# Issuing the second pieces of q and k ahead of a distance table, with new orders for all engines

## The chip, the cores and the metric

The kernel runs on one core of a Trainium2 chip. The metric is device microseconds (us) of one execution; a median of several executions is quoted. Executions of this program scatter more than the change is worth, so runs are also told apart by the mean clock granted to TensorE, which every execution records: "clean" below means a mean clock of 0.998 or more.

## The reference, cut to what matters

Attention with a window of 128 positions and a distance bias, over 8 batches, 8 heads, 576 positions and 64 dimensions, and behind it a two-layer MLP with h·cos(h) between its layers:

```python
scores = scale * np.matmul(q, k.transpose(0, 1, 3, 2))
rel = pos[:, None] - pos[None, :]
bias = slopes[:, None, None] * (-np.abs(rel))[None]
mask = (rel >= 0) & (rel < 128)
attn = softmax(np.where(mask, scores + bias, -1e9))
x = (attn @ v).transpose(0, 2, 1, 3).reshape(4608, 512)
h = x @ w_in                    # 512 -> 2048
out = (h * np.cos(h)) @ w_out   # 2048 -> 512
```

## The kernel before: the parts concerned

POOL issues all casting loads (float32 in memory, bf16 on chip). It also builds two small tables at the start: an identity, which TensorE needs for transposes, and the distances, from which ScalarE makes eight masks. q and k of the first batch come in two pieces each; q's first piece comes over SP without a cast and is cast by VectorE and ScalarE.

```python
        def distances():
            op("pool", lambda e: e.iota(dif[:, :, :], ...), w=["dif"], occ=450)
            op("pool", lambda e: e.affine_select(dif[:, 0, :], ...), r=["dif"], w=["dif"], occ=430)
            op("pool", lambda e: e.affine_select(dif[:, 1, :], ...), r=["dif"], w=["dif"], occ=400)

        def masks():
            for h in range(H):
                op("act", lambda e, h=h: e.activation(EM[:, h, :], dif[...],
                    ACTF.Exp, scale=slopes[h]), r=["dif"], w=[("EM", h)], ...)
        ...
        load_first_q()
        warm(9, 512, "warm")
        load_qk("k", k, 0, 0)
        distances()
        identity()
        load_qk("q", q, 0, 1)
        load_qk("k", k, 0, 1)
        constants()          # memsets on VectorE, among them those of v's buffers
        load_v(0, range(2))
        load_w_in(0)
        load_v(0, range(2, NBLK))
        masks()
```

What an engine does in which order is not the order of this source. A packed table holds a start for each of the 2,762 operations and, for 50 copies, the engine; operations are sorted by it, and the waits follow from the data:

```python
        raw, n = zlib.decompress(base64.b85decode(STARTS)), len(self.all)
        for i, o in enumerate(self.all):
            code = (code + 256 * raw[i] + raw[n + i]) & 0xFFFF
            o.start = code >> 1
            if len(o.eng) > 1:
                e = "dve" if code & 1 else "act"
                o.fn, o.eng = o.fn[e], (e,)
        self.order = sorted(self.all, key=lambda o: (o.start, o.seq))
```

The softmax here doesn't subtract the row's maximum and nothing guards it: scores larger than these inputs give would overflow.

## Time and profile before

| | value |
|---|---|
| Time | 304.05 us median of 3 (303.7 to 304.66); 303.8 us of 5 with two later runs |
| Span of the profiled run | 301.0 us, TensorE clock 1.000 |
| TensorE idle ahead of 17.2 us / 17.2 to 57 / 57 to 281 / behind | 4.55 / 0.18 / 1.38 / 2.78 us |

The profiled run took 302.76 us, a microsecond less than the timed ones. That was no reason to doubt its order of events.

### The profile page before, as it was taken

What the parts mean: (1) busy time and instruction counts of PE and PEld (TensorE: products, weight loads), DVE (VectorE), ACT (ScalarE), POOL (GpSimd) and SP (SyncE); (2) the same over time, 40 slices, a digit from 0 to 9 for tenths busy, and PEclk for the clock granted to TensorE, in tenths of its full rate; (3) what the DMA queues carried; (4) which work ended last, traced back from release to release, by engine and by line L of the source; (5) the groups of instructions that cost most, each with busy time, mean ns of one, the idle gap of its engine ahead of it and who ended that gap; (6) DMA issues with size and microseconds to landing.
All of it is one profiled execution on the core that took longest, in us unless ns stands there. A gap on an engine that the chain in (4) does not pass through costs nothing.

```text
span 301.0 us, 7132 instructions
## 1 busy us (share of the span) xinstructions
PE 292.1 (97%) x2897; PEld 199.4 (66%) x2917; DVE 244.1 (81%) x511; ACT 210.1 (70%) x304; POOL 94.9 (32%) x122
## 2 busy tenths in 40 slices
PE   7789999999999999999999999999999999999996
PEld 3478745546774588547898886468655865666685
DVE  3787888679977998999978989898878976886871
ACT  6977777487877686787768866888666955744431
POOL 6930992058969301870195014000000000000000
PEclk9999999999999999999999999999999999999999
DMA  7999999999999999999699989645014004310123
GB/s 140 183 200 211 206 169 145 143 130 238 158 138 206 145 156 157 202 166 126 132 141 134 168 85 134 140 84 122 11 53 116 10 2 113 107 35 2 35 89 122
DMA packets 148064, 38.02 MB, mean 126 GB/s; under 512 B 133696, under 2 KB 146752, under 8 KB 148032
## 3 DMA queue, kind: packets, MB, share of 16 engines
q0 software_dynamic: 99344, 18.10, 78.9%
q1 hardware_dynamic: 48688, 19.47, 32.8%
q8 instruction: 23, 0.38, 0.5%
q14 instruction: 9, 0.07, 0.1%
HBM read 36.70 MB, written 9.44 MB: 153 GB/s over the span
## 4 chain that ended last, share of the span: by engine, by line
PE 93%; DMA 4%; POOL 1%; issue 1%; DVE 0%; ACT 0%; ACTq 0%
PE ps L738 36%; PE ps L879 34%; PE ps L762 5%; PE ps L823 5%; PE ps L506 5%; PE ps L593 3%; DMA vp<-in_v_dram 3%; PE ps L596 2%; DMA ob<-in_q_dram 1%; PE ps L700 1%; POOL vp L329 1%; PE ps L451 1%; PE ps L497 1%; PE ps L580 1%; PE ps L582 1%
## 5 line engine op out<-in xcount | busy, mean ns | idle before, releaser
L738 PE MATMUL ps<-xT,w_inb 128*128 128x512 bf16 (+1 forms) x557 | 126.9, 355 | 0.8
L744 ACT ACTIVATE cos<-ps,halfpi 128x512 f32<-128x512 f32 x128 | 82.3, 687 | 39.9 <-PE ps L738 24.3
L748 DVE TENSOR_TENSOR gT<-ps,cos 128x512 f16<-128x512 f32 x128 | 83.0, 686 | 21.4 <-ACT cos L744 20.3
L738 PEld LDWEIGHTS ps<-xT,w_inb 128*128 128x128 bf16 x576 | 55.3, 98 | 39.7 <-DVE gT L748 2.0
L538 ACT ACTIVATE p<-ps 128x768 bf16<-128x768 f32 (+1 forms) x64 | 55.6, 915 | 10.7 <-PE ps L506 7.8
L329 POOL DMA_DIRECT2D vp<-in_v_dram x40 | 34.0, 880 | 66.7 <-PE ps L596 50.9
L879 PE MATMUL ps<-wsum,gT 128*128 128x256 f16 x256 | 48.8, 273 | 0.1
L562 DVE TENSOR_TENSOR p<-p,emask 128x512 bf16<-128x512 bf16 (+2 forms) x96 | 41.9, 460 | 3.5 <-ACT p L538 3.0
L879 PE MATMUL ps<-w_outb,gT 128*128 128x256 f16 x256 | 41.8, 273 | 0.1
L879 PE MATMUL ps<-wsum,gsum 128*128 128x256 f16 x256 | 38.2, 273 | 0.1
L879 PEld LDWEIGHTS ps<-w_outb,gT 128*128 128x128 f16 x256 | 24.6, 98 | 8.3 <-issue 0.5
L339 POOL DMA_DIRECT2D qnat<-in_q_dram x30 | 25.4, 894 | 14.9 <-DMA qt<-qnat 14.9
L879 PEld LDWEIGHTS ps<-wsum,gT 128*128 128x128 f16 x256 | 24.2, 98 | 7.3 <-issue 0.6
L339 POOL DMA_DIRECT2D knat<-in_k_dram x30 | 25.6, 921 | 7.8 <-issue 5.2
L879 PEld LDWEIGHTS ps<-wsum,gsum 128*128 128x128 f16 x256 | 24.5, 98 | 5.2 <-DVE ob L903 0.2
L879 PE MATMUL ps<-w_outb,gsum 128*128 128x256 f16 x128 | 26.2, 273 | 0.0
L593 PEld LDWEIGHTS ps<-vp,p 128*128 128x128 bf16 x256 | 16.2, 97 | 5.5 <-issue 1.5
L593 PE MATMUL ps<-vp,p 128*128 128x65 bf16 x256 | 18.3, 193 | 1.5 <-DMA vp<-in_v_dram 0.8
L506 PE MATMUL ps<-qt,kt 64*128 64x128 bf16 (+1 forms) x320 | 18.8, 239 | 0.8 <-ACT kt L468 0.6
L899 ACT ACTIVATE qrows<-ps 128x512 f32<-128x512 f32 (+1 forms) x18 | 9.9, 550 | 12.3 <-PE ps L879 12.2
L596 PE MATMUL ps<-vp,p 128*128 128x65 bf16 x192 | 17.1, 193 | 0.0
L823 PE MATMUL ps<-w_outb,gT 128*128 128x512 f16 x64 | 16.9, 380 | 0.0
(80 smaller groups left out, 338.6 us busy)
## 6 DMA issues: line engine op xcount, KB each, us to landing
out_dram<-ob SPq DMA_DIRECT2D x32, 256.0 KB, 3.0
vp<-in_v_dram POOLq DMA_DIRECT2D x32, 128.0 KB, 8.6
qnat<-in_q_dram POOLq DMA_DIRECT2D x24, 128.0 KB, 10.6
knat<-in_k_dram POOLq DMA_DIRECT2D x24, 128.0 KB, 12.2
w_inb<-in_moe_w_in_dram POOLq DMA_DIRECT2D x4, 512.0 KB, 9.7
w_outb<-in_moe_w_out_dram POOLq DMA_DIRECT2D x4, 512.0 KB, 21.1
out_dram<-ob SPq DMA_DIRECT2D x8, 128.0 KB, 1.7
qrows<-in_q_dram POOLq DMA_DIRECT2D x1, 576.0 KB, 14.4
```

The source lines that it names most:

```text
L329: op("pool", [lambda e, t=t, rows=rows: e.dma_start(vp[b % 2][0:rows, t, :, 0:64], v[b, :, 128 * t:128 * t + rows, :].rearrange("h p d -> ...
L339: fns.append(lambda e, t=t, rows=rows: e.dma_start(nat[which][b % 2][0:rows, t, :, :], src[b, :, 128 * t:128 * t + rows, :].rearrange("h p ...
L506: ins = e.matmul(ps[:, banks[x], c0:c1], keys_ap(b, x, pr, kc), query_ap(b, x, pr, qb, 128 * nb), start=True, stop=True)
L538: op("act", lambda e: e.activation(P[i][:, :, 0:hi], src_[:, :, 0:hi], ACTF.Exp, scale=0.125), w=held + [("P", i)], occ=920 if G else 691, ...
L562: op("dve", lambda e, p=p, m=m: e.tensor_tensor(p, p, m, ALU.mult), r=[("P", i), ("EM", h0), ("EM", h1)], w=[("P", i)] if n != 1 else [("P ...
L593: ins = e.matmul(o, P[i][:, x, d0:d0 + 128], V[:, kc, h, 0:65], start=True, stop=not two)
L596: ins = e.matmul(o, P[i][:, x, p0:p0 + 128], V[:, kc - 1, h, 0:65], start=False, stop=True)
L738: op("pe", lambda e, kc=kc, c0=c0: e.matmul(ps[:, bank, c0:c0 + n], w_in[:, kc, 128 * fc:128 * fc + 128], xT[:, kc, (r0 + c0) % XR:(r0 + c ...
L744: op("act", lambda e: e.activation(cosb[ci][:, :], ps[:, bank, :], ACTF.Sin, bias=halfpi[:, 0:1]), r=["halfpi"], w=[("B", bank), ("cos", c ...
L748: op("dve", lambda e: e.tensor_tensor(gT[gi][:, fc, :], ps[:, bank, :], cosb[ci][:, :], ALU.mult), r=[("cos", ci)], w=[("B", bank), ("g", ...
L823: op("pe", lambda e, t=t, fc=fc, bank=bank: e.matmul(ps[:, bank, :], gT[gi][:, fc, 128 * t:128 * t + 128], w_out[:, fc, :], start=(fc == 0 ...
L879: op("pe", lambda e, t=t, fc=fc, bk=bk: e.matmul(ps[:, bk, 256 * t:256 * t + 256], lhs(fc, t), rhs(fc), start=first and fc == 0 and (last ...
```

## The change

The intent is to have the DMA engines supplied earlier: q's and k's second pieces are issued right behind the identity, and the distance table, which only the masks need, moves behind them. A new table of orders was searched for this.

```diff
         load_qk("k", k, 0, 0)
-        distances()
         identity()
         load_qk("q", q, 0, 1)
         load_qk("k", k, 0, 1)
+        distances()
         constants()
...
 STARTS = (
-    "c-oy-4RBLc7S2lxT%Iys&+bUL4K=-eREdvR$|Ftk@{+dDG!%%4ONa<1RB<XGcAzd=...
+    "c-o~_3v?7k7M%_O>$I}lyrVd&jB%(mF^)}$p`BmNBm)V<BtVRC3?U#pXoN{bfe~0_...
```

The second hunk may reorder every engine and changes the engine of 20 of the 50 copies.

More of the change, by code (lines that the diff above doesn't have):

```diff
@@ L30 @@
 STARTS = (
-    "c-oy-4RBLc7S2lxT%Iys&+bUL4K=-eREdvR$|Ftk@{+dDG!%%4ONa<1RB<XGcAzd=`B^Hu{8ZiHZ-uQ;cKiW%1ckLIGs}YF2"
-    "#AU-u&lG{=<Yg*E24uf{YkRtB~6<))WW{Wym#NZ=bm@YcfNB@3_>hwNM7A5Lu^n-n=r67DUKOpg1#Gz{}LKW)eQY67zVUo?v"
-    "%z-%orlwg2Y}l`JQ|gqA9NtgVBIL!O(gYuVU9NyV`E#8uj|K5=+7niwWIoT|pXp1|92yCjKVqXSxtbsJ15_MuRaSh#F(U4~A"
-    "aXz?R;U0c}0sg;em8l1NG*3Fo3hA`GDmk{-J$lGrs!QmGN^vF;nr%(&x%u|sG{SQFZN#}?}?$ZYFZB~4(A^p>PDJ%P}GD}6w"
-    "q1Jo0~zToKV9=(cxoeb&C7$KD}X%=G1WOv3Rv<nHb&>|$1+LKhe4lL4C(yug?v_uJmQt^v)d7VH`FhtU<MXwXlRDva|$<Woi"
@@ L36 @@
-    "1Y>)*ae{QpXzw~I47hC6A6REs&=tMh`sdj-(5l}vMnlgJ>AC6TSx@aq-!dU}SNPepKfi0Z#@!UPST}c#LR<1|rXG{f(Up#jN"
-    "H@WaMxBX<%m@M<(-k`U1#Lj<|3S#K@)df2D5F!7O2}9mA%!#@!!=8~9PMgJ8A5CKMrKD6rG!$n(?er(f{L+7e?b`rUAcY^ru"
-    "E03wHI$@gPQwj^c``9jyNttnvS7ISNyqp?(S+CvG%UDu{-3p&VLpC(_>J}^<yBUA$b+1xAmFg&VeZOO@s7K6-oJSr;cFM|IE"
-    "bN`b~3s0MY(SB6<yymLBf(c0BR7BYKswC-i9HJ$EC$EX3j+wYRqsp{Gx%FGSL`dY_A?B`(^>_`I5I%Fx)iL%GD`*Ckh8p2d{"
-    "y%An-ZV~Z|~-@3x@FY@~rnhHESs{<#(GlcJF2rZ`2y*Kf)!Jift6}eq_+v~^c%TLEI_$j+|k<&L<jsXSpD8HG$ku~S-Jrxf*"
@@ L41 @@
-    "MmLtSoI-j<8tyvD+W2=veT(ON>3L<A_nDC^ZS!|EP2W=p%~F;<$`0je$LG!u<mKiO5D5`s#&aw6C;sZxPk=xX5N1*%1ejf<Y"
-    "_<BN2+R$P*k`{<WFj$&yWfbMFp+>sohEXwA2O9{1V|N=t4wM;eTx&Zf&QlSZQU-~W2O557quKuJjV!71;Dhpn9(T=Z7x>@iL"
-    "x*en@n1Sh$h_^lRECTw|9DD58nNs^^4yf7_QiCALl#EyyK?qgr{<LWVPqpr<;9Db4sV_#No$^HZO0A)WnMM?XIlPZ1w9KGlI"
-    "EJ1Z1T7;_#Owf!$RIQm#=4a{HdkjXbQcz8D-L;cV(V2*F8+C@AO_<@CS6bpPn2DwI^yO78dBfCt>bk1z0r763ozF8CTep7CY"
-    "|9PB<jK;`GBRsrT$eMI6QYa>G7s8_Qpchit}C2dlEU3?7YNmsNV_+yGqYo{E3rM^cMpGEyg&_~^BDfLmm_Avy54{Cqmz%8o4"
@@ L46 @@
-    "c(77yRjOEtcbc0s$vf@D(PeD6`SDS3H<v4qZeRz@b4Nj$L>0d?zpM~fCdEHGe?lRYN+xL?n}q?tAp8B*{>($G!dsfRHaEJOZ"
-    "~WI$MZuitSpgz4!pu?#xX21n1So=GuU)3V;>?J1f=H&1NP;PWgoK&Sic}={R-~UHk~r#y5+ZV7;d~+?ZOoqMM>;D|5r|EODK"
-    "iMG2?t6}Eu}J8)HfO6z0B%>dgr5X>0pt%21L5hd(YBS8)tgA&;W3CWe^luTZc*bvpO5^3$-OOSGYP0gSBZl)N*ds)&!|!QMF"
-    ")@aqT-AWO?e7TkR9fluf(0WUKrH+d1JGtE04fujlYs=`>8pI+iuRpnORA;6mjzl;)htu4ru9v3k1Bkekc~_Hse^=6d_`KNNy"
-    "I`>R{w%Yd@dzW7$U=IOWmtNeA2XTvMVsi$izYW_X(XeCoHW*r>_K{ORfjEG8*Bmv8M|Msr6D6;}4xpY2*I3DXDenetCaT?-U"
@@ L51 @@
-    "W<o|gS>>XH2s5w^HeUQ@ww)ElO@t|ksFHW|sF~`>y@|whc|Z1*(|Ye7Gk@Sg?|iseIYk{C1=^(E1i)u#o3JD;(^ep*r+)Auq"
-    "dcI^RVX;LdnBvWsP6Y!CClt_vcma<IViDspW_TI-*e*l3+A=uv%HS`#_m|&)P8b%v1@<bM#VpT-jYIi;$<V^$L2LGaf0;Zr@"
-    "2sEE!&^6e{H>Q42}G=1hAag=^5ddI&PV_+vRsWRM%7&u$pOtYS>2>5b!W4=mZAXFy~qz-893s=?DWif{=%_6m_snp&}v&MPf"
-    "?=I?Nd)uLFrQE8iuOl1clVdu5T92gm{95<`%;@i9~0C5i^{qg<WLWvYYB)yETkNL;JtSedJlouftSJ{RGVjXrBrhXRpH(C#F"
-    "41jWXNN#M>6EPg_=s}Ji336U-89f%Xbn&Ij+Cb}7ZN75d(N?0%WwZDzzdV3^b(UxEj&^_j*ld0&2^GxRIFMxQ^5c+c8R{Nu7"
@@ L56 @@
-    "S~donmwuR~wJH7~HFLa<B}Y!#{X@38&*Vy<1vRkmYpy)L%X+~6*E?Y(U2S#TVW;Iw?xdsXxz7>mSL+{Mf8v&a<J_sk7d#bG0"
-    "v^2~6K1OwITA*+iwW?v_P2Su8A+H2Osf+SiIC6`O%<Y!s-6zfhaos}UNNBNW;A1V=o<x7M}BfpS2f2o7SeD2rRR}~90^H*JA"
-    "aSOqux1d)l_QHBG|#2oDWH!kbU9+L`U&%=L%}>K~1~bD$yX8I4G<{`<8NPrnVn-xcXiQnW~QE%8wpx7}C|I&OYC?J^Xl~!<p"
-    "HD)LXcw5MoDW<Rb|enOn=iew%4De0iwy=oULwrrim%+>^2=2Vco?eE;_spI^=#nHwLGt4Kgegcc98;VZVblaNf84jaA*Gbg8"
-    "z&~z3-6kTy<f<CcK3mFHgR&Q@aw21{oed+<d`e8G^$~CtK^570<T^=&_AOuXLx`|}NjdG?DBjW03Ks}a;w;@dRrEB1iZNB36"
@@ L61 @@
-    "+fUH-+Aiv!SE3H)`T#fsRB|})vih*&{YeU99kxJ4*rvYArS<MNa<JxQwfF)Dn>MZisCE7_SsxE`8_HW6cNIGh&0JHrSt;Li="
-    "!5&=9k{hFTiRnjQ~1mB5&Mq+c<?ul3n$00T7Chlv8<$c&e_v?7pjUkAidd$!`?p$z*v$VNSZhXxO5{%qKtKGGT><x*r!q^i#"
-    "60gY(r*zcr0f!c0MIc?Dww=l3J;{L1K)ZJZaUZMnU#P*}qd=7V_EaSBwGf=IRCodv@u_<p$tCE&IIE;wf7fa@X<0^LL}%JD6"
-    "3Wj#^vA3e+K0Um+Q84zjf~)lJO99nKw92f>r|iKklT_s<DRSdGm!18oi4@=lJkda9VaE`&p}LY7F_RPR<~9AN<#WLTLp%W}F"
-    "f;bhVHc~n7K2RwvT_+%_uJE<1KL{XS%TCMopdiaVj&JLdAJVBUZ$5{!A6~Y|EIbZ0-&$uKr8CwAI-Bch~)XMehTn^P-T~@Tz"
@@ L66 @@
-    "TBQA!ZBs1j`wZ|t+;=uusm`{_hxnEa60hRwh}}USR|mh|xGi5@_u{<W7WHt5!RyDKsISIh_CdoU#wWi4Z*iaV<5L{lO#Ol*`"
-    "2k0!Z92LQIzJ`dJDIN9Y+Vm-QIW`5F{t?6JLNgKn_}g97G+r<BN(`c1&)7&)Dv-B$u+fc)*lbN3W?;N?#y^=ZY+1NPIavH1D"
-    "ykZaPD`xzl)DJBEHi(`zimL{|^uA{Jj"
+    "c-o~_3v?7k7M%_O>$I}lyrVd&jB%(mF^)}$p`BmNBm)V<BtVRC3?U#pXoN{bfe~0_v#^HGLJXi7CH^2HBJ28J`M7FSR7Auzi"
+    ">`PMD)?FS99B_8k|mkxecj0<nM?@iHl(NORn@C{_uY4^O@bCR#hzFzDnu_Z4LqqOM~tp!(zK43spEgAsq-12zXU-OPMJDJyG"
+    "FE5pIUcU(+yf&S3rvpGe%5F#&6Q;gj4l!eBQRcM$dPi)^96f>ViXy3f+TUK??Ex_?UZoi}ePy7=cHHq$I;%TQatPH1&QW2^O"
@@ new lines @@
+    "tae}Jjg)c4bK!)TW`!4wg?M|;lc-=g*2U5i1e^=S8%0HKFT5F)~9wCJ7oq;rJU(~YU$Ap5fjNoV4^-LPssAdUm*EFfy}tAw*"
+    "d7Qeoe16pEPbn`{)>S^6W#(6tWlXONuxu9u6i;kjBnHaLa0G)FilG}P);_)*m7dcDZ9r(4!VE#V{ro|J?*tM+_n`EuW83*8="
+    "$!EHk4mzc89Ua&%w4zMuwl?8htQz#+Ux8CER0I<_)th;J>Pw`Lb42=R3H`3^f7EoIqwzE~c!-XZP4ReKaJtJ=QY6~LYnxudT"
+    "2iY{OZ;n3P_N#|Cq;gFg(m<lm=Y-(O(<wBR?0%mA|%X7w3yCfF~!QV>om#H_IMI@6sj?)>zYk!F?DkAoO~M8`pY?ZK}&+x#p"
+    "eL?Gq5G$8t8fpv5GY%jK*Icf~h~Pi>cRu_HIiL6+I)IF9yFxuY^QixA&I&<kLd$ghu1FUq~cRzZN0h4<e8h!7$s-eSb&KX-E"
@@ new lines @@
+    "t)p|FI+vN_$?oiFI0cikzBBz_SjUWbCQs`K<h*V?FHeB)@5gwsZPom=a?pW<gldkI%GAqK4vFwSNxxl}uTDU+G;{NSb*k0(P"
+    "ue9_kjYX@!n!8R%o@C5?1%#Evp&F1C<({f&|`0Ww%oY7al^-RnAKA+Fy#@B)XK5wroS^Ag2O-gFoo%RzFNRV%~o4>i{LS<7%"
+    "C7V_^mZgr8TIC_G!+9UbZx(uvjCNqxk#;JzFvt7Sq?-p%gk$PuG}qE#|FL!Rdk5wDUrKIDL_#)9-3V?{PAb5bpD#*i$x=e&U"
+    "Z!Q(0+RVer9Mey#ijf`4-pl#nfX_SjewayrcxlF+iv%hDr`}6-lK}TfGHC7Ei1%nB}6PW^Vx(_oJMN-ql}^twxYy)t-gZ~f@"
+    "VHIbQXxE)JAy<j){a3%5S;$#FoOA6_dYuYF2YJ=)T`MuHa+JZ?!!sy-gQ2R@j_^&Hv=@Mq-pHsah(p-uc(;@AQ~cu0BrvWr2"
@@ new lines @@
+    "wel@2(KV?yeE@<Mvtaj`t?OC89~_pBBd1@+dz%a0ZWWfh8nNq#r@3lLSXwg**^=1IT+W_cvY0&7kaG((t45RjIFAEb|G<$RC"
+    "9;ABs@gsSDa^o5zO8MuP+9l8fTL@BY?@tdovPfpL<99mbFoHt%%Px-uuB`CJ?JE#gpd7CBh*Lip8#Ncz$DdQjd{fimDQ<Bx3"
+    "i8la~m1}QjAla_lh&!?T$@NaJ{g`d^NICzC!?X6kOdnj7KLW-Me?tunuAb|FadMMdv?jaIfwnbrO1Z-Ua{B&2U_t;w|M>cwl"
+    "Qr2(-C5bo-9!XEbz;ZMJe`GALM#&K2Fzs2Yg;jim{c(~%S<~P8BBDG7EcB>5pjuObE37>BBi=2GIS19=&8#BwiGH4*NKoT>R"
+    "z1+k@p6bO*yTQ15WQ0P?_p|`hJk=_*by0sg6&%e~y0zANe_BVSX1vW94^-WQ1chm0<d3D*;&8yRrcB$kQZx(G2hJK`mf;&p*"
@@ new lines @@
+    "s$tM|TK%2?i7Spuu~x(Ds~RHFIU<o?|@lO0IgZ*x9NS4_G?XUHhue^M*eMMs`lt1~2(wx(^_&=|SxgwBu=sozmc)xNcM%j)|"
+    "a)HZzR<?s$k8=ILwOuAvrvA~OgP}-j0(|51VdCr-A>{a5Uo-if&&j5u|(gi3oLL{lKOh14e1FuvP-K+I6nt|_9Std|UC4yxp"
+    "i&!|iv49K{P8wbeNM$N-Yd*YiyAu}?5M_6k?x#%NTM9Z!c7P;jB8rG#{!Q6X8ybB_(e~^bu1RyC+IuBZWfFe^-&s@F<9p0|F"
+    "G~<&-a-{Tncij6!;s0pP!QuO*B46)b6tg8m%Yzo)mr)F1N&aHO|Q=z0rS)UR=smq_8(l%!4<bv?|!x62#2X@uVfburqk&Vhb"
+    "*TK9cCW=C!5`|ry;j;1i0GUKMe!}wdEDTKVCevrosJb)u<ci?UZRJ%McdxLAn@7iJW8Lgk_(8XBx;on8-x)TSTP9LyWjHkdm"
@@ new lines @@
+    "~D`f##aM3{_u>4*0D#Vj`>Pn}|c1gny7ncajd!ACp*+uf1^#Ixk6o)%qU_`OvBC8Cv2F?J$iolBb_PKO1aqdxwwU-CiCPET&"
+    "$2oy3&A@-cH!!Re5D8$F75h61@h?U<?j0kLuUr9t8#oeuZIVzMcUW`9ZsG`#$C+{c85KP?dE?kKGz--NA$Ve)xR<04MhmEJ2"
+    "+~B;-;+y?%$<t7o`e?(}bzd~jbior9TkJ&_*3kLskS;l>{a>{<=jQS~^pO$pNMp6lxt=~3oIes=6*U%Au2135^`33T&X0oY_"
+    "l9XViju{A>~lOdR%WbzQxBQD+PU?_CKBI^q@&mku(6re)I$+0_>;0ZD`wed7sGaG-O~>o=;S#R>*lN|6<^nNiC-n@wEPTpua"
+    "?ivT_w%pvtdESK`-|)**@L{Okw=D@&>T+M{vHKJ5))w@*Nb_())obsc!Fwj3UhMNEY-nMGbAekq-;%p0E3M=LgLXIlxu0JEv"
@@ new lines @@
+    "%Hc&bC*xG4!qm|0{IMuY519wlG0)#khvuZ4vp&4RNoZOw`)mpj*vug?xOI2)RNBI4HIjGzuX6|pwWbC7Tps7J>Mjbh5Kqd;W"
+    "Z6*~pwAQ*M%Hdsi;n3q^+mac_v1P01IkTQOs&ORLoH~wURG~eq4X7g0*k}y>CC^;VA$q-&1R`1VD52;Y1P`B|!bEwwG1uA3k"
+    "H_^;>S>AgV17&<=h^dS}4}Pim-Hr1UydD+;3)%A?fQyiEZ8rT<N%5<y;yv^X!^&S{fOYe?J9jj`^rloHE!*Z%i@e#(9JW^Z`"
+    "U;pcMP2Sf;os#+8#6C>cT*dswwjZ=up2>xIom@G6!Zu&2s+%g!MJfdK>(uCMnl?kqlXj$@zVm7C8~&itfon5Ra4r=6p@nZ;`"
+    "%b10zpztgDI}lqKW`6E+e^&R?HJsb3qBfM_GJ5qiWqhCo(8y{JSM|>lm*C8q^67%`f+iDdB|=*A%ny_lBzKQT0`}lkxPudVF"
@@ L69 @@
+    "o+(wbcFCG3+jJHJA$$NFglH95z7p+u2RZzx;k+*_Ml56*J3MW$zETS=&PiA^jGVk((_e(L{{(V(i!ZYkZA;`$!zjw<-+QZI!"
+    "SEN}XW$Y6#{6j4t;^@I5p2ADr87Uwb<^GL5a{<(okkcb|f1frVqeyKhev9S{sFD2A8wMq#+wU5sYQk#9;vKr=Rk5}UD$M`s_"
+    "vc&pWUbx7gG4-L^u$1xGPr*_s-gU?iwIA`rMZ4>)-WE{HqWm%%Jjh&YhVCz7eEHW((8?dE`^|3a^&`S&i4_)=LU!qdrsi)*v"
+    "Em06a`h8fh*I&QsqS?WT7bk7QGH-f$&jn3txO`Iq8efyVc@b<;y<{BVjsh19d`?PuIdFtenn|PxFhF6`p?4~!4NokPfRh=KO"
+    "4TC81rC%Ojy`4_CHg`1$z"
 )
```

## The prediction

> **What bounds the kernel now.** I read the page first: the busy shares, then the chain that ended last.
>
> ```profile
> PE 292.1 (97%) x2897; PEld 199.4 (66%) x2917; DVE 244.1 (81%) x511; ACT 210.1 (70%) x304; POOL 94.9 (32%) x122
> PE 93%; DMA 4%; POOL 1%; issue 1%; DVE 0%; ACT 0%; ACTq 0%
> ```
>
> TensorE is busy in 292.1 of 301.0 us, and the chain runs over it for 93%. The rest, 4% DMA and 1% POOL, must lie at the start, since the change touches only POOL instructions there. So I asked for busy time by stretch, with the cuts at 17.2 us and at later stage borders:
>
> ```profile
> core 0: us, PE busy (x) PEld busy (x) DVE busy (x) ACT busy (x) POOL busy (x), PEclk, DMA share, GB/s
> 0.00:17.20 17.20, 12.65 (x174) 6.68 (x175) 10.13 (x32) 14.17 (x24) 14.80 (x27) 1.00 1.28 164
> 17.20:57.00 39.80, 39.62 (x452) 26.62 (x454) 32.89 (x79) 27.20 (x41) 17.29 (x21) 1.00 1.66 183
> ```
>
> From 17.2 to 57 us TensorE is idle for 0.18 us: the stages behind the start are full. Of its 8.9 us of idle time, 4.55 lie ahead of 17.2 us and 2.78 in the last 20 us; the drain at the end is not touched in the source. The first 1.26 us precede the dummy matmuls that keep the clock up, so about 3.2 us of idle between 5.3 and 17.25 us is all that a better start could give. Whatever makes the dense stretch begin earlier, with the same work done ahead of it, ends the kernel earlier by as much.
>
> The chain in order of time says what the dense stretch waits for:
>
> ```profile
> 5.66 0.28 DVE vp L395
> 5.94 0.29 issue
> 6.23 1.76 POOL vp L329 x2
> 7.99 0.76 POOL w_inb L361
> 8.74 0.84 POOL vp L329
> 9.59 7.57 DMA vp<-in_v_dram
> 17.16 0.09 issue
> 17.25 0.19 PE ps L593
> ```
>
> It is a later tile of v, issued by 9.59 us and landing at 17.16 us. A 7.57 us transfer of 128 KB is no latency: it is the queue in front of it. So the question is whether the DMA engines were ever empty before. The DMA view of the first 18 us, in 40 slices of 0.45 us, answers it:
>
> ```profile
> DMA  0000093999999499999999999999999999999999
> GB/s 0 0 0 0 0 146 86 355 419 282 207 212 101 40 151 193 202 188 196 202 191 156 155 155 170 204 209 207 205 209 200 148 145 154 153 191 205 204 212 205
> ```
>
> There is one hole after the start: the thirteenth and fourteenth slices, 5.4 to 6.3 us, move 101 and 40 GB/s where neighbours move about 200. The first piece of k has drained, and the second piece of q has not begun. POOL's timeline shows why:
>
> ```profile
> 1.33 0.82 POOL L310 DMA_DIRECT2D krows<-in_k_dram  x1 [0.81 <-POOLq L1056]
> 2.24 0.37 POOL L381 IOTA dif<- 128x256 f32 x1
> 2.77 0.29 POOL L385 TENSOR_SCALAR_AFFINE_SELECT dif<-dif 128x128 f32<-128x128 f32 x1 [0.15 <-POOL dif L381]
> 3.20 0.29 POOL L388 TENSOR_SCALAR_AFFINE_SELECT dif<-dif 128x128 f32<-128x128 f32 x1
> 3.44 0.20 POOL L374 MEMSET ident<- 128x128 bf16 x1
> 3.71 0.29 POOL L375 TENSOR_SCALAR_AFFINE_SELECT ident<-ident 128x128 bf16<-128x128 bf16 x1
> 3.95 0.75 POOL L310 DMA_DIRECT2D qrows<-in_q_dram  x1
> 4.70 0.71 POOL L310 DMA_DIRECT2D krows<-in_k_dram  x1
> ```
>
> The reader sees POOL build the distance table and the identity between the issue of k's first piece and that of q's second. ScalarE's rows beside it show the first three masks at 3.53 us, as soon as the table is there (1.03 us for the three).
>
> **What the skill says.** (1) "DMA: Bandwidth & Descriptors", Latency and other measured facts: a software-generated DMA has its first byte after about 1 us. Here it is longer: q's second piece is issued at 3.95 us and packets pick up in the slice that starts at 6.3 us, about 2.3 us later. I use 2.3. (2) The same page, Issuing engines are not separate DMA queues: all issues share the same 16 engines and interleave. The trace agrees: between 4 and 5 us both queues move packets, 154 software and 63 hardware. An early second piece can therefore take bandwidth from q's first piece, but as both software pieces stand in one queue I expect it behind k's first. (3) "Perfetto Trace Analysis", on the GPSIMD lifecycle: time such instructions by the spacing of their starts, not by reported spans. So the table costs 3.44 - 2.24 = 1.20 us, not the sum of its spans (0.95). (4) "ScalarE: Activation LUTs", What ACT_TABLE_LOAD costs: an ACTIVATE with immediates takes 186 ns + 0.833 ns per element and overlaps the next by about 93 ns. For 256 elements that is 399 ns; the trace's median for a mask is 400 ns, and three take 1.03 us. It agrees.
>
> **The change part by part.** Nothing is added or taken away. Two DMA issues pass ahead of three POOL instructions, and a new order with new engine choices for the copies stands in an opaque table.
>
> *Issues earlier.* With the table gone from in front, the identity starts at 2.24 us, takes 3.95 - 3.44 = 0.51, and q's second piece is issued at 2.75 us (1.20 earlier), k's at 3.50. First packets at 2.75 + 2.3 = 5.05 us, while k's first piece still drains until some 5.6. So the hole should close. What it is worth is not the 1.20 us but the work missing from the hole: against 200 GB/s, 0.45 x (1 - 101/200) + 0.45 x (1 - 40/200) = 0.22 + 0.36 = 0.58 us. From there on the DMA engines are backlogged, so all that follows shifts by this: q's second piece from 8.45 to 7.9 us, k's from 10.2 to 9.6, and the tile of v from 17.16 to 16.6. The issues of v do not move in the source order (POOL still does the same work by 5.4 us and then waits 0.81 us for a memset of v's buffer until 6.23); they needn't, as the queue before them is full.
>
> *What it is worth on TensorE.* It waits 0.76 us for that tile just before 17.25, 0.34 us for q's and 0.29 us for k's second piece. 0.58 fits below 0.76: gross gain 0.58 us.
>
> *Table later.* Identity and two issues in front (0.51 + 0.75 + 0.71 = 1.97 us) move its end from about 3.5 to 5.5 us. The three masks that ScalarE did at 3.53 to 4.56, in a time when it had nothing else, must go behind its cast of q at 4.78 to 5.41. From there to the table load at 18.27 us ScalarE has hardly a gap: 0.4 us at 12.96 is the only one named. So 1.03 us of work is added to a full stretch. Some can be taken off: a copy out of PSUM of 0.57 us (128x512) or 0.89 us (128x640) can go to VectorE, which was busy 10.13 of the first 17.2 us and stood idle 1.4 us before its first mask product at 8.87. And ScalarE waits 3.4 us for TensorE in the first 30 us once the first layer of the MLP runs, so later delay can be absorbed. I take 0.15 us as what remains on the path: my estimate between 0 (all moved) and 1.03 (none).
>
> Sum: -0.58 + 0.15 = -0.43 us. In the scale of the timed runs, 304.05 - 0.43 = 303.6; I go to **303.5** as a search that was made for this order should not have ended on a bad start.
>
> **Rivals.** *ScalarE takes the place of the DMA.* The masks push the first exponentials (8.03 us) and the xT copies (15.72) back; then the dense stretch waits for exponentials rather than v. For it: ScalarE's full stretch. Against it: only the first two of eight masks are needed for the first product at 8.87 us, and the rest can fall into later gaps. It would make 303.7 to 304.5. *The transfer is hidden anyway.* The product that the waiting matmuls read also needs VectorE, whose mask multiply at 15.26 lasts 1.28 us, until 16.54. If v comes at 16.6 and VectorE has not moved, the gain is capped at some 0.7 us; that leaves 0.58 standing but bars more. If VectorE is later, the gain goes to zero: 304.0. *The new order changes the full stages.* With TensorE at 39.62 of 39.80 us there is little to win there, but the last 51 us have about 3 us of idle (0.21 and 2.78) and a new order can take or give some tenths. It goes either way: 302.8 to 304.6. *Contention with q's first piece*, which lands at 4.75 us and starts everything: early packets of the second piece could push it back. Against it: they would come at 5.05 us by the 2.3 us above. If not, +0.3 us.
>
> **Range and chances.** The known part gives -0.58 to +0.3 us; the new order widens it by some 0.6 either way; the runs before spread over 303.7 to 304.66. So 302.6 to 304.6 for 8 in 10. 2% is 6 us, more than all idle time at the start together, so faster by 2% is nearly excluded; slower by 2% would need a broken order. Faster 0.01, same 0.98, slower 0.01.
>
> **What would show it.** In the changed trace q's second piece is issued near 2.75 us and lands by 8.0; the hole at 5.4 to 6.3 us is filled; the masks start at 5.4 us or later; v's waiting tile lands near 16.6 and the dense stretch starts with it. If v lands earlier and TensorE is still idle until 17.2 with ScalarE or VectorE named, the second rival holds. If the start gains 0.5 us and the time doesn't move, idle time in the later stages, above all the last 20 us, has grown. The prediction fails if the hole stays because descriptors come later than 2.3 us, or if the search moved v or the weights in the queue too.

## The result, and the profile after

The changed kernel took **303.02 us** (302.86 to 303.51, 5 runs) against 303.8 us (303.7 to 304.66, 5 runs). The ratio is 0.9973, 95% interval 0.9955 to 0.9990. The predicted 303.5 was within half a microsecond and the range held it. Whether it was for the reason given is another question, and the profile after raises it at once.

POOL did what was foretold. This is its timeline after; columns are start, duration, engine, line, operation:

```profile
1.33 0.85 POOL L310 DMA_DIRECT2D krows<-in_k_dram  x1 [0.82 <-POOLq L1056]
2.17 0.23 POOL L374 MEMSET ident<- 128x128 bf16 x1
...
2.71 0.76 POOL L310 DMA_DIRECT2D qrows<-in_q_dram  x1
3.47 0.71 POOL L310 DMA_DIRECT2D krows<-in_k_dram  x1
4.20 0.37 POOL L381 IOTA dif<- 128x256 f32 x1
...
6.00 0.89 POOL L329 DMA_DIRECT2D vp<-in_v_dram  x1 [0.53 <-DVE vp L395]
```

q's second piece is issued at 2.71 us (2.75 foretold), k's at 3.47. The DMA view of the first 18 us, in slices of 0.45 us, shows the hole of 5.4 to 6.3 us filled, 179 and 142 GB/s where there were 101 and 40:

```profile
DMA  0000094999999999999999999999999999999999
GB/s 0 0 0 0 0 137 105 328 400 291 205 200 179 142 142 168 185 185 185 183 182 168 151 149 105 112 152 184 191 198 165 178 160 186 146 153 188 189 205 209
```

But a new dip stands further right, 105 and 112 GB/s around 11 us, where the kernel before had 170 and 204. And TensorE did not gain at the start. Its longest waits after are these (time in all, times, longest):

```profile
PE ps L762 <- DMA w_inb<-in_moe_w_in_dram: 1.7, 1, 1.7
PE ps L416 <- DVE p L413: 1.3, 1, 1.3
PE ps L506 <- DVE kt L469: 1.2, 1, 1.2
PE ps L451 <- DMA krows<-in_k_dram: 0.7, 1, 0.7
```

The wait for v, 0.76 us before, is gone; in its place stands one of 1.7 us for the second quarter of w_in, which landed at 20.5 us. Busy time by stretch (columns as in the prediction) sums it up:

```profile
0.00:17.20 17.20, 13.15 (x180) 7.42 (x181) 10.28 (x34) 12.92 (x22) 15.17 (x27) 1.00 1.26 158
17.20:57.00 39.80, 38.12 (x445) 26.07 (x444) 33.17 (x77) 29.84 (x43) 17.05 (x21) 1.00 1.60 192
57.00:281.00 224.00, 223.97 (x2150) 152.27 (x2149) 189.74 (x384) 160.01 (x225) 62.82 (x75) 1.00 1.11 115
```

Idle ahead of 57 us: 4.05 + 1.68 = 5.73 us, against 4.73 before. Idle from 57 to 281 us: 0.03 against 1.38 us. Two single profiles thus say that the start, which the change was for, became worse and the late stages, where I expected nothing certain, became better. That is what the experiments had to test.

### The profile page after: what moved, and what is told of

The parts are those of the page before. It is cut to its first block, busy times and chain, and to the rows that moved or that the text cites. A ratio compares the mean times of both kernels' runs of the same rounds, so it can differ in the third digit from the quotient of the medians.

```text
span 301.2 us, 7145 instructions
## 1 busy us (share of the span) xinstructions
PE 292.4 (97%) x2917; PEld 199.9 (66%) x2917; DVE 245.1 (81%) x513; ACT 209.1 (69%) x302; POOL 95.0 (32%) x122
## 4 chain that ended last, share of the span: by engine, by line
PE 92%; DMA 5%; POOL 2%; issue 0%; DVE 0%; ACT 0%; ACTq 0%
PE ps L738 37%; PE ps L879 33%; PE ps L823 5%; PE ps L506 5%; PE ps L762 4%; DMA w_inb<-in_moe_w_in_dram 3%; PE ps L593 3%; PE ps L596 2%; DMA ob<-in_q_dram 1%; POOL vp L329 1%; PE ps L451 1%; PE ps L700 1%; PE ps L497 1%; PE ps L580 1%; PE ps L582 1%; PE ps L662 0%
## 5 line engine op out<-in xcount | busy, mean ns | idle before, releaser
L738 PE MATMUL ps<-xT,w_inb 128*128 128x512 bf16 (+1 forms) x576 | 129.0, 355 | 0.0
L879 PE MATMUL ps<-wsum,gT 128*128 128x256 f16 x256 | 48.0, 273 | 0.0
L879 PE MATMUL ps<-wsum,gsum 128*128 128x256 f16 x256 | 39.4, 273 | 0.0
L879 PE MATMUL ps<-w_outb,gsum 128*128 128x256 f16 x128 | 24.9, 273 | 0.0
L593 PE MATMUL ps<-vp,p 128*128 128x65 bf16 x256 | 18.3, 193 | 0.2 <-DVE p L562 0.2
L762 PE MATMUL ps<-xT,w_inb 128*128 128x256 bf16 x128 | 16.3, 273 | 1.7 <-DMA w_inb<-in_moe_w_in_dram 1.7
L506 PEld LDWEIGHTS ps<-qt,kt 64*128 64x128 bf16 x320 | 11.0, 94 | 9.7 <-issue 4.0
## 6 DMA issues: line engine op xcount, KB each, us to landing
knat<-in_k_dram POOLq DMA_DIRECT2D x24, 128.0 KB, 10.4
```

What stands on the lines that cost most here:

```text
L506: ins = e.matmul(ps[:, banks[x], c0:c1], keys_ap(b, x, pr, kc), query_ap(b, x, pr, qb, 128 * nb), start=True, stop=True)
L593: ins = e.matmul(o, P[i][:, x, d0:d0 + 128], V[:, kc, h, 0:65], start=True, stop=not two)
L738: op("pe", lambda e, kc=kc, c0=c0: e.matmul(ps[:, bank, c0:c0 + n], w_in[:, kc, 128 * fc:128 * fc + 128], xT[:, kc, (r0 + c0) % XR:(r0 + c ...
L762: op("pe", lambda e, i=i, fc=fc, kc=kc: e.matmul(ps[:, bank, 256 * i:256 * i + 256], w_in[:, kc, 128 * fc:128 * fc + 128], xT[:, kc, r0:r0 ...
L879: op("pe", lambda e, t=t, fc=fc, bk=bk: e.matmul(ps[:, bk, 256 * t:256 * t + 256], lhs(fc, t), rhs(fc), start=first and fc == 0 and (last ...
```

## The experiments

Twelve runs were made; all gave correct results. Times in us, median and range of all runs; "clean" is the count with a clock of at least 0.998 and their mean.

| Run | chip | median (range) | clean: count, mean | ratio to before (interval) |
|---|---|---|---|---|
| before, beside the next four | A | 304.21 (302.28-305.91) | 7 of 11, 303.82 | |
| after_again | A | 302.69 (302.14-304.52) | 5 of 6, 302.63 | 0.9961 (0.9922-1.0000) |
| undo_issue | A | 302.19 (302.0-303.1) | 5 of 6, 302.15 | 0.9940 (0.9902-0.9979) |
| new_start_old_rest | A | 303.43 (302.9-304.02) | 6 of 6, 303.43 | 0.9977 (0.9942-1.0012) |
| old_start_new_rest | A | 303.18 (302.49-303.67) | 6 of 6, 303.09 | 0.9966 (0.9931-1.0001) |
| before, beside the next four | B | 305.74 (302.57-307.45) | 2 of 11, 302.95 | |
| move_only | B | 304.05 (303.27-304.6) | 6 of 6, 303.99 | 0.9961 (0.9918-1.0005) |
| undo_again | B | 302.51 (302.27-303.4) | 6 of 6, 302.64 | 0.9917 (0.9877-0.9956) |
| after_third | B | 302.79 (301.95-304.75) | 4 of 6, 302.39 | 0.9934 (0.9885-0.9983) |
| undo_v4late | B | 302.20 (302.06-302.7) | 6 of 6, 302.30 | 0.9905 (0.9867-0.9944) |
| before, beside the next four | C | 304.12 (302.96-305.27) | 8 of 11, 303.89 | |
| after_hoist | C | 302.43 (302.05-302.9) | 6 of 6, 302.48 | 0.9949 (0.9922-0.9976) |
| after_hoist_v4late | C | 302.02 (301.87-302.55) | 6 of 6, 302.10 | 0.9933 (0.9905-0.9962) |
| before_fill | C | 304.36 (303.77-304.72) | 2 of 4, 304.25 | 1.0009 (0.9975-1.0042) |
| before_again | C | 305.04 (one run) | 1 of 1 | |

### First, what makes the runs scatter

The kernel before had a mean clock of 0.994 in 4, 9 and 3 of its 11 runs on the three chips, so the ratios of chip B compare mostly slowed runs with clean ones and are not used below. What happens then is in one profile of the changed kernel, **after_again**, whose run took 304.52 us. It is the changed kernel unedited.

> The changed kernel once more, as the anchor for the others of this call and to see how far a profile repeats. All theories: ratio to the kernel before 0.996 to 0.999, 303.0 us. Theory START (closing the hole in the DMA lets the dense stretch begin earlier): TensorE idle ahead of 57 us would be below the 4.7 us of the kernel before. Theory LATER (the start is no better, the new order of the later stages has less idle time): idle ahead of 57 us again near 5.7 us and idle from 57 to 281 us again near 0.

Its busy time by stretch; the third number from the right, ahead of DMA share and GB/s, is the granted clock:

```profile
19.00:20.00 1.00, 0.00 (x0) 0.00 (x0) 0.99 (x3) 0.99 (x2) 0.00 (x0) 1.00 1.27 211
20.00:21.00 1.00, 0.43 (x4) 0.35 (x5) 0.00 (x0) 0.20 (x1) 0.00 (x0) 0.92 1.23 203
21.00:22.00 1.00, 1.00 (x6) 0.71 (x5) 0.00 (x0) 0.00 (x0) 0.00 (x0) 0.50 1.25 208
22.00:23.00 1.00, 1.00 (x9) 0.83 (x7) 0.00 (x0) 0.30 (x2) 0.00 (x0) 0.50 1.23 205
23.00:24.00 1.00, 1.00 (x7) 0.67 (x6) 0.87 (x3) 0.67 (x2) 0.00 (x0) 0.50 1.22 214
24.00:25.00 1.00, 1.00 (x21) 0.91 (x20) 0.62 (x2) 0.28 (x1) 0.00 (x0) 0.87 1.20 225
```

TensorE waited 1.97 us for w_in, and then had half its clock for over 3 us; 0.08 + 3 x 0.50 + 0.13 = 1.7 us of clock are lost. In the other profile of a slowed run (before_fill, below) the clock is lowered for as long, but earlier, from about 17.8 to 21.2 us, behind a wait of 0.72 us for v that had shorter gaps ahead of it. new_start_old_rest waited 1.99 us for w_in and kept its full clock. These are the rows of TensorE behind those two waits, of before_fill and of new_start_old_rest, with the idle time in brackets:

```profile
17.64 0.19 PE L595 MATMUL ps<-vp,p 128*128 128x65 bf16 x1 [0.72 <-DMA vp<-in_v_dram]
```
```profile
20.47 1.16 PE L755 MATMUL ps<-xT,w_inb 128*128 128x256 bf16 x9 [1.99 <-DMA w_inb<-in_moe_w_in_dram]
```

So idle time at the start can cost its own length and, now and then, 1.7 us more, but the length of the last wait alone does not decide it, and what does stays open. The kernel before had the lowered clock on each of the three chips, in 16 of 33 runs, and before_fill, which is nearly the same kernel, in 2 of 4. All the other kernels together, the changed one among them (3 of 12), had it in 4 of 60; move_only had it in none of its 6 runs beside the 9 of 11 on chip B. So it goes with the kernel before, and 1.7 us in a run that has it is twice what the new rest is worth below. Which part of the change avoids it was not tested, and means of clean runs leave it out. The five runs of the changed kernel behind the result above were all clean; of the five of before the clocks are not on record.

The expectation of idle time ahead of 57 us failed in a way that teaches: 57 - 13.72 - 37.83 = 5.45 us, and 224 - 222.97 = 1.03 us later on. At half clock TensorE is busy for longer (the nine matmuls behind the wait took 1.88 us, and 1.16 in the profile after), and the modelled ends of matmuls differ a little from profile to profile. Busy time in two stretches is too coarse here; a mark in the order of work is better. I used the third load of an activation table on ScalarE, which stands between the first MLP stage and the attention behind it at 38 to 41 us.

### Splitting the kernel in time: new_start_old_rest and old_start_new_rest

The two tables were spliced: operations that the first table starts in its first 40 us keep its order, everything else has the other's.

```diff
-        self.order = sorted(self.all, key=lambda o: (o.start, o.seq))
+        # FIRST, REST: the two tables; 1600 of their units are about 40 us
+        for o in self.all:
+            early = FIRST.start(o) < 1600
+            o.key = (0, FIRST.start(o)) if early else (1, REST.start(o))
+            o.eng = FIRST.eng(o) if early else REST.eng(o)
+        self.order = sorted(self.all, key=lambda o: (o.key, o.seq))
```

(The result was written back in as a table of ranks; this is what it holds.)

> All that the new table starts in its first 40 us in the new order, everything after in the old order. START: keeps the whole gain, 303.0 us (ratio 0.997). LATER: no gain or a small loss, 303.8 to 304.5 us (1.000 to 1.002).

> The old order and the old issue order for the first 40 us, the new order for the rest. START: no gain, 303.8 us (ratio 1.000). LATER: keeps the whole gain, 303.0 us (0.997) or a little more, since the old start had 1.0 us less idle time in the profiles.

With before and after_again, on one chip, this is a square of four; means of clean runs:

| | old rest | new rest |
|---|---|---|
| old start | 303.82 | 303.09 |
| new start | 303.43 | 302.63 |

The new rest is worth 0.73 and 0.80 us, the new start 0.39 and 0.46 us. By the scatter of the runs, differences from the corner of both olds (302.28 to 305.91 us) are uncertain by about 1 us and the others by about 0.6 us, an estimate; only the 0.80 stands clear of that. **The larger part came from behind 40 us**, where the move of two DMA issues has no part; a smaller part from the start is likely, but not shown.

The spans confirm the first of these without the scatter of the start. From the third table load to the end, these ACT rows (start, duration) of before, changed kernel, new_start_old_rest and old_start_new_rest

```profile
38.70 1.28 ACT L538 ACT_TABLE_LOAD   x1
```
```profile
39.25 1.28 ACT L538 ACT_TABLE_LOAD   x1
```
```profile
39.15 1.28 ACT L531 ACT_TABLE_LOAD   x1
```
```profile
39.53 1.28 ACT L531 ACT_TABLE_LOAD   x1
```

give, taken from the spans of 301.0, 301.2, 301.7 and 301.4 us: 262.3 with the old rest, 261.95 with the new, 262.55 with the old, 261.9 with the new. Over all profiles, the new rest took 261.9 to 262.0 us in eight of nine (263.0 in undo_again, where TensorE waited 1.0 us for a transposed k of a later batch), the old rest 262.3 to 263.4 in four with a full clock. That gap of some 0.4 to 0.8 us fits the square. The start's part (38.3 to 39.3 us at the mark with the new start, 38.7 to 39.9 with the old, slowed runs aside) overlaps from run to run; the square makes it likely, no more.

### The issue order alone, inside the new orders: undo_issue and undo_again

The changed kernel, with the table put back ahead of the identity on POOL. Nothing else differs, on any engine.

```diff
+        by = {o.w[0]: [] for o in self.all[13:21]}
+        for o in self.all[13:21]:
+            by[o.w[0]].append(o)
+        first = by["ident"][0].start
+        for i, o in enumerate(by["dif"]):
+            o.start = first - 3 + i
         self.order = sorted(self.all, key=lambda o: (o.start, o.seq))
```

> The new order on every engine, with the distance table put back ahead of the identity on POOL alone. START: the hole at 5.4 to 6.3 us is back, k's second piece lands later by about 0.5 us, and the time grows by 0.4 to 0.6 us, to 303.5 us (ratio to the kernel before about 0.999). LATER: what POOL does first is hidden, the time stays at 303.0 us (0.997).

> The new orders with the distance table back in front on POOL, a second time, beside the changed kernel. START: slower than after_third by 0.4 to 0.6 us. ORDER: as fast or up to 0.5 us faster than after_third, ratio to the kernel before 0.994 to 0.997.

> The changed kernel, third set of runs, beside undo_again. Ratio 0.996 to 0.998 by both theories; the time from the third ACT table load to the end 262.0 us within 0.2, as in all profiles with the new order there, against 262.3 to 262.6 with the old one.

On chip A the kernel without the early issue was faster than the changed one (302.19 against 302.69, clean means 302.15 and 302.63), on chip B its clean mean was slower (302.64 against 302.39) and its median lower. Together: **no gain from the early issue** that these runs can see. Weighted by their scatter, the 20 clean runs put that gain between about -0.7 and +0.2 us, an estimate that leaves the predicted 0.58 outside. The early issue was meant to be the cause, and it can be taken out without loss. The third set of the changed kernel put its mark as expected: third table load at 38.30 us, 300.2 - 38.3 = 261.9 us to the end.

Yet the hole was there again in undo_issue (slices of 136 and 65 GB/s) and TensorE's wait for w_in's second quarter had not grown: 1.3 us. Why does filling the hole not help? The DMA between 10 and 12 us, in slices of 0.05 us, first without the early issue (undo_issue):

```profile
GB/s 156 156 148 159 154 151 144 159 164 151 141 159 159 154 154 161 156 159 164 179 179 161 213 174 184 223 138 246 195 192 233 184 225 246 143 266 184 184 205 205
DMA packets 1639, 0.36 MB, mean 178 GB/s; under 512 B 1472, under 2 KB 1639, under 8 KB 1639
```

and with it (new_start_old_rest):

```profile
GB/s 133 120 125 131 125 143 128 136 169 102 182 128 74 123 10 10 64 128 82 95 59 95 120 69 146 169 123 220 133 192 184 184 225 205 143 225 205 184 184 205
DMA packets 863, 0.27 MB, mean 137 GB/s; under 512 B 678, under 2 KB 863, under 8 KB 863
```

The packets under 512 B are v's. By the packets in the traces, with the early issue its first two tiles start about 0.6 us sooner and are nearly through by 10.6 us; then, until 11.2 us, the engines move 10 to 128 GB/s, before the large packets of w_in come at their full rate. Without it v's tiles are through at about 11.2 us and w_in's packets follow at full rate at once. **The hole did not go, it moved**, from 5.4-6.3 to about 10.6-11.2 us (to 11.9 in the profile after). All 14 profiles, old and new orders together, say the same. By 8 us the seven with the early issue have moved 1.27 MB on average and the seven without it 1.15, which is the 0.12 MB of the hole (0.58 us at 200 GB/s); by 12 us 1.87 and 1.85, by 18 us 2.96 and 2.97. What was won at 6 us is lost again by 12 us. The tile of v that the kernel before waited for landed at 17.1 to 17.9 us in the four profiles with the new start and the early issue, and at 16.4 and 16.6 us in undo_issue and undo_again.

The packets in the traces, which no view prints one by one, show what a hole is made of; q's second piece and w_in are told apart by their sizes, 1280 and 1024 bytes. Without the early issue the first 32 packets of q's second piece took 252 to 321 ns each on average, and with it 116 to 148; the first 32 of w_in took 97 ns without it (146 in before_again), and with it 137 to 342. A packet that takes longer counts as busy for longer, so the row of busy tenths can read 9 over a hole.

### The move alone, in the old orders: move_only

```diff
+        for o in self.all[14:17]:                       # the distance table
+            o.start = 193                               # behind k's second issue
+        late = {("EM", 3): 369, ("EM", 5): 397, ("EM", 7): 427}
+        for o in self.all[:60]:
+            if o.w and o.w[0] in late:
+                o.start = late[o.w[0]]
         self.order = sorted(self.all, key=lambda o: (o.start, o.seq))
```

In the old table three masks stand ahead of ScalarE's cast; they were moved with the distance table, or the cast would have stood behind masks that wait for it. v's first issue came at 6.34 us, 0.1 us later than in the kernel before.

> The kernel before with the move alone: distance table behind both issues on POOL, and the three masks that ScalarE did before its cast put between the first exponentials, all other orders and engines as before. START: most of the gain without any search, ratio to the kernel before 0.997 to 0.999 (303.0 to 303.6 us on a chip where before is 303.8). ORDER (the gain is in the new orders of the engines, part in the first 40 us, about 0.4 us after them; the issue time itself gives nothing or costs): ratio 1.000 to 1.003.

Its six runs were all clean: 304.05 us. The kernel before has only two clean runs on that chip, 302.57 and 303.34; over all three chips its 17 clean runs average 303.75. The ratio of 0.9961 fell on the first theory's side, but only as nine of before's eleven runs there had the lowered clock. Clean against clean, the move alone gained nothing that these runs can see; whether it is what avoids the lowered clock, in all six of its runs, is the rival left open above. In its profile the DMA has the same dip (77 and 94 GB/s at about 10 us), and TensorE's wait for v is still 0.9 us.

### Does an earlier supply of v and w_in cure the dip? after_hoist

If the dip is there as the descriptors of v and w_in come no earlier than before, then issuing these earlier should fill it. POOL's first issue of v waits 0.53 us for a memset on VectorE that stands behind a cast; it can go ahead of it.

```diff
+        for o in self.all[21:23]:    # memsets of v's first buffer
+            o.start = 60             # ahead of VectorE's cast of q
         self.order = sorted(self.all, key=lambda o: (o.start, o.seq))
```

> The changed kernel with the two memsets of v's first buffer put ahead of VectorE's cast of q, so that POOL's first issue of v needn't wait for them: it comes at about 5.45 instead of 5.97 us, and all issues behind it too. Theory SUPPLY (the early second pieces only move the hole in the DMA from 5.4-6.3 to about 10.6-11.6 us, as the descriptors of v and w_in come no earlier): that second hole is refilled about 0.5 us sooner, w_in's second quarter lands 0.3 to 0.5 us before the 20.5 us of the changed kernel's profiles, and the clean runs fall from about 302.75 to 302.3 us. Theory BACKLOG (my prediction: the DMA engines are busy from 6 us on whatever is issued): landings and time as after, 302.7 us.

POOL's first issue of v came at 5.58 instead of 6.00 us, so the lever was 0.4 us. The dip was not filled sooner; this is the DMA of the first 18 us:

```profile
GB/s 0 0 0 0 0 123 114 364 423 278 200 212 199 210 202 191 202 202 210 156 156 152 158 96 97 105 143 198 193 163 206 159 156 151 161 173 182 203 209 209
```

The slices of 96, 97 and 105 GB/s lie where the dip was, and 2.95 MB were moved by 18 us, no more than without it. w_in's second quarter landed at 19.9 us against 20.5, 20.5, 20.4 and 19.6 in the four profiles with the early issue, which is no clear step. **The supply theory, in this form, fell as well.** The clean mean of 302.48 us lies between the changed kernel's on the other two chips, 302.63 and 302.39: nothing to build on. What limits w_in's first packets in the dip stays open. The profile shows that they start slowly there and not what they wait for; no run separates what VectorE and POOL do at that time, which is an untested rival.

### A shorter queue in front of w_in: undo_v4late and after_hoist_v4late

As TensorE waits for the second quarter of w_in at 20 us in every profile with the new start, one can put something behind it that isn't needed yet: v's tile of 64 rows, first read at about 33 us in the new orders (28 us in the old).

```diff
+        first = {}
+        for o in self.all:
+            first.setdefault(o.dma, o)
+        first["ldv04"].start = first["wi1"].start + 1
```

> As undo_again, with the 64-row tile of v issued behind the second quarter of w_in, as TensorE waited 1.3 to 2.0 us for that quarter at about 20 us. If the DMA queue sets the start: that wait shrinks by about the tile's time, some 0.5 us, and the kernel ends 0.3 to 0.5 us before undo_again, ratio 0.993 to 0.995. If the wait is taken over at once by another (ScalarE or the next quarter): within 0.1 us of undo_again.

> The same with v's 64-row tile behind w_in's second quarter as well. SUPPLY: w_in's second quarter lands near 19.5 us, TensorE's wait for it (1.7 us) mostly goes, 302.0 us, the best so far. BACKLOG: 0.5 us from the tile's move alone, 302.2 us.

undo_v4late took 302.20 us beside 302.51 for undo_again, a clean mean lower by 0.34 us: as the queue theory had it, at the low end, and the scatter of both is about as large. TensorE's wait for w_in fell from 1.1 to 0.8 us. after_hoist_v4late took 302.02 us beside after_hoist's 302.43, lower by 0.38 us in the clean means, though its profiled run still shows a wait of 1.6 us there. This is the **fastest version seen**, ratio 0.9933 to the kernel before (0.9905 to 0.9962; clean means 302.10 and 303.89), 0.7 to 1.0 us below the three medians of the changed kernel, which was not run on that chip. Yet the landings don't show the queue at work: w_in's second quarter came at 19.81 us against 19.69 in undo_again, and at 19.85 against 19.91 in after_hoist. The cause of this gain, if it is one, is not shown.

### What the new rest does better: before_fill

One difference of the late stages can be pointed at. Near 209 us the old order puts the scores of a tail (L497) straight behind a block of attention products. The rows of TensorE in the kernel before and in new_start_old_rest, with the idle time in brackets:

```profile
208.68 0.41 PE L497 MATMUL ps<-qt,kt 64*128 64x64 bf16 x16 [0.31 <-issue]
```
```profile
209.45 0.41 PE L490 MATMUL ps<-qt,kt 64*128 64x64 bf16 x16 [0.54 <-issue]
```

In the changed kernel the same row has no bracket, as six matmuls of the MLP's second layer stand in between:

```profile
209.16 0.41 PE L497 MATMUL ps<-qt,kt 64*128 64x64 bf16 x16
```

So three such matmuls were moved ahead of it in the kernel before, on TensorE alone.

```diff
+        for o in self.all[1988:1991]:   # three products of the second layer
+            o.start = 8283              # ahead of the tail's scores, at 8284
         self.order = sorted(self.all, key=lambda o: (o.start, o.seq))
```

> The kernel before with three matmuls of the second layer moved ahead of the tail's score matmuls near 209 us, where its profile has TensorE idle for 0.3 to 0.6 us in every run of the old order and in none of the new. If that idle time is what part of the later gain is: the wait is gone or below 0.2 us, and the time from the third ACT table load to the end goes from 262.3-262.7 to 262.0-262.3 us. If it only moves: 262.3 to 262.7 as before.

The wait fell to 0.24 us and the time from the third table load to the end was 302.7 - 40.3 = 262.4 us, at the low end of the old order's 262.3 to 263.4, where the kernel before stands with the wait. By the terms set before the run this is idle time that only moved: no part of the gain is shown here, and the run's time (304.36, with two of four runs slowed) can't show so little. Where in the later stages the gain sits is open.

### before_again

> The kernel before once more, for a second profile of it. All theories: span 301 to 302.5 us with the clock at 1.00, or about 2 us more with the clock at 0.994; if so, the lowered clock lies between 15 and 30 us, where TensorE waits for the first weights.

One look: 305.04 us with a full clock, span 303.3, so above the expected 301 to 302.5. It has the wait at 209 us (0.6 us), another of 0.6 us for a transposed k of a later batch, and 1.1 us for w_in at the start. It shows that scatter of 2 us is possible without the lowered clock; in this profile some of it is DMA that lands late (w_in's second quarter at 21.26 us against 19.87).

## Why the prediction was right or wrong

The number came out right by luck: 303.5 foretold, 303.02 measured, a gain of 0.8 instead of 0.55 us. Its reason was mostly wrong: the term that was to make the gain measured about zero, and one counted as going either way made most of it. By its steps:

- **The issues come 1.2 us earlier and the hole closes**: right, 2.71 us against 2.75 foretold, and the slices read 179 and 142 GB/s. But the hole had been misread: "the second piece of q has not begun" is wrong. By their size its first packets stand at 5.44 us in the trace of the kernel before, 1.5 us after the issue and just as k's first piece ends (5.50 us in the profile after); they came slowly, 35 of them before 6.3 us against 84. So 2.3 us was the time to the full rate in that trace, not to the first packet. (A small slip: the idle time between 5.3 and 17.25 us is 3.3 us, not 3.2.)
- **"From there on the DMA engines are backlogged, so all that follows shifts by this"**: this is the step that failed. The DMA row reads 9 in every slice, and I took busy engines for engines at their rate. The time won at 6 us was lost again from 10.6 us on, where 10 to 128 GB/s were moved. q's second piece landed at 8.7 us in the profile after (7.7 to 8.7 in all seven with the early issue), not safely by 8.0, and k's at 10.4 (9.5 to 10.4) instead of 9.6. The shift had gone when it came to v: its tile landed at 17.88 us instead of 16.6, and the bytes by 18 us are unchanged. So the term of -0.58 us measured about zero: undo_issue and undo_again lost nothing without it, move_only gained nothing with it.
- **"The issues of v ... needn't [move], as the queue before them is full"**: the queue in front of w_in was the weak place. That issuing v 0.4 us earlier did not cure it says that I don't know its cause either.
- **The wait for v, 0.76 us, is what the dense stretch hangs on**: right for that profile and overtaken by the new order, which puts MLP matmuls ahead of the products that need v. The wait for v went, and one of 0.8 to 2.0 us for w_in's second quarter came in its place.
- **Masks later, +0.15 us**: not seen as a cost of its own. ScalarE began the masks at 5.51 us as foretold; the new order moved a copy of q to VectorE. The first exponentials came later, as the rival on ScalarE had it (8.96 us against 8.03, and 8.63 in undo_issue), but nothing measures the 0.15.
- **"The new order changes the full stages ... goes either way"**: it is here that most of the gain lies, 0.73 and 0.80 us in the square. I had counted 1.38 us of idle time from 57 to 281 us only in part, named the last 51 us and not the waits ahead of them, and treated the re-search as noise around a mechanism, when it was the larger part of the change.
- **Contention with q's first piece**: it landed at 4.88 instead of 4.75 us, about 0.1 us; small, as given.

What my list of signs said: "if v lands earlier and TensorE is still idle until 17.2" did not come about: v landed later, not earlier, and the idle time lay at 20 us, behind another transfer. A sign that looks only at the wait one knows can miss the one that takes its place.

## What to carry to other kernels

When a change moves one thing and re-searches all orders, treat these as two changes: splice the old and new orders at a point in time, and undo the one thing inside the new orders, before crediting either. A filled hole in a DMA view is worth something only if the bytes moved by the time of the next wait have grown; compare the cumulated bytes, not the busy row. And for effects below half a per cent, sort the runs by granted clock first, ask which kernel has the lowered runs, and measure from a mark in the order of work to the end rather than by idle time.

## What the Trainium skill lacked or had wrong

- "DMA: Bandwidth & Descriptors", Latency and other measured facts, gives about 1 us to the first byte of a software-generated DMA. For k's first piece, the first one on its queue, the first packet came 2.8 us after the start of the issue and 2.0 us after its end (issued 1.33 to 2.15 us, first packet at 4.16; 4.0 to 4.2 us in all 14 profiles), while q's first piece was moving on the hardware queue. Behind a filled queue it can't be seen.
- Slow first packets, on no page with their times: where one transfer followed another on the same queue, the first 32 packets of the next took up to 342 ns each on average, against 97 ns for the same packets in six of the seven profiles without the early issue, and the engines moved 10 to 128 GB/s from 10.6 to 11.2 us, while the row of busy tenths in slices of 0.45 us says 9 there, with a single 7. The cause is open; no run here tests a reason that a page may give.
- "TensorE: Matmul & The Clock Gate", HAM oscillation, warns of gaps over about 3.4 us. Here the clock fell to 0.50 behind a gap of 1.97 us in one run and behind one of 0.72 us, with others ahead of it, in another, and gaps of 1.99 and 1.68 us in two more runs had no such result. So the size of a single gap does not tell it here. The length of the slow stretch, about 3.4 us in both, agrees with that page's window.
